# Layer norm, grouped attention and GEGLU on one core: a recorded schedule with clustered half-depth passes, a ones column in V, and the attention output transposed by DMA

## The chip, the cores and the metric

One core of one Trainium2 chip. The metric is the device time of one execution in microseconds. A ratio compares a kernel with the kernel before, by fast runs of the same rounds on the same chip; it is not quite the ratio of the medians that are quoted beside it. The kernel before itself falls into two groups of executions, near 632 and near 635.5 us, so a single ratio is good to about 0.4%, some 2 us. Traces give a span from first to last instruction, which is some 2 us shorter than the device time.

The profiles shorten the names of the engines: PE is TensorE (matmuls; PEld its weight loads), ACT ScalarE, DVE VectorE, POOL GpSimd, SP SyncE. Both kernels let TensorE write its results into PSUM banks of 128 x 512 and have another engine copy a bank out before it is written again. A pitch is the time from the start of one matmul to the start of the next.

## The reference

```python
x  = A_x                                   # 1 x 2048 x 448, bf16
xn = layernorm(x)                          # no weights
q  = (xn @ wq)                             # 448 -> 16 heads x 256
k, v = last 512 of 2048 cached positions   # 8 kv heads, each used by two q heads
p  = softmax(q k^T / 16)                   # no mask
s  = (p v) @ wo                            # 4096 -> 448
b  = (gelu_tanh(xn @ w_gate) * (xn @ w_up)) @ w_down   # 448 -> 1792 -> 448
out = x + s * silu(b)
```

448 is three full contractions of 128 rows and one of 64. The remainders of 64 are done two at a time, on the upper and lower half of the array: a half-depth pair.

## The kernel before

Two stages: the feed-forward (56 units of 128 hidden columns by 512 tokens), then attention (64 steps of one head by 512 tokens). A feed-forward unit on TensorE:

```python
def gate_up(n):
    ...
    for kt in range(nk_full):            # 3 full-depth passes for gate, 3 for up
        pe.matmul(G[n % 2], lhsT=wg[:, kt, cols], rhs=xnT[:, kt, toks], ...)
    ...
    pe.matmul(G[n % 2], lhsT=wg[:HALF, kt, cols], rhs=xnT[:HALF, kt, toks], ...)   # half-depth pair
    pe.matmul(U[n % 2], lhsT=wu[HALF:, kt, cols], rhs=xnT[HALF:, kt, toks], ...)
# then down(n - 3): four matmuls of 448 columns
```

GELU is written as g * sigmoid(2k(g + c g^3)): ACT copies both banks and takes a sigmoid, DVE does four operations a unit. In attention the output is kept feature-major (oT), so the softmax divisor has to be spread over all partitions. POOL sums the exponentials, TensorE multiplies the sum by ones, DVE inverts a whole bank:

```python
pool.tensor_tensor(esum2, expT[0:2], expT[2:4], ALU.add); pool.tensor_tensor(esum, ...)
pe.matmul(DEN[:, :], lhsT=ones[:, :], rhs=esum[:, b, :])          # 512 columns, each head
pe.matmul(O[e], lhsT=vv[:, g, j, e * P:(e + 1) * P], rhs=expT[:, b, j, :], ...)   # 8 per head
dve.reciprocal(rden[:, b, :], DEN[:, :])
dve.tensor_tensor(oT_buf[:, c, :], O[e], rden[:, b, :], ALU.mult)
```

At the start POOL waits for the last x, then issues w_gate, w_up and w_down, and TensorE waits for all of them:

```python
pool.wait_ge(s_xl[last_slot0], 16)
...                                      # w_gate, w_up, w_down
pe.wait_ge(s_wgu, 16 * n_wgu); pe.wait_ge(s_wd, 16); pe.wait_ge(s_tpe, NT)
```

The softmax here doesn't subtract the row's maximum and nothing guards it: scores larger than these inputs give would overflow.

Of the kernel before, what the change touches and what calls it, by code (L numbers as in the profile page):

```python
# [6 lines left out]
ALU = mybir.AluOpType  # L7
# [3 lines left out]
GELU_C = 0.044715  # L11
GELU_SQ_SCALE = GELU_C ** 0.5
GELU_K = 2.0 * 0.7978845608028654
LN_EPS = 1e-5


class _Chain:

    def __init__(self, eng, sem):
        self.eng = eng  # L20
        self.sem = sem
        self.cnt = 0

    def mark(self, ins):
        ins.then_inc(self.sem, 1)
        self.cnt += 1
        return ins

    def wait(self):
        if self.cnt > 0:  # L30
            self.eng.wait_ge(self.sem, self.cnt)


def bass_recurrent_scan__sliding_block_cached__geglu_ffn__prompt_kernel(
# [12 lines left out]
    P = 128  # L47
# [4 lines left out]
    rep = Hq // Hkv  # L52
# [5 lines left out]
    TPC = QC // P  # L58
    kts = []
    o = 0  # L60
    while o < D:
        kts.append((o, min(P, D - o)))
        o += P
    NKT = len(kts)
    NF = F // P
    NJ = W // P
    NE = Dh // P
    NCO = HD // P
    att_scale = float(Dh) ** -0.5
    assert S % QC == 0 and F % P == 0 and W % P == 0 and Dh % P == 0 and D <= 512  # L70
    assert TPC == 4 and NF >= 3 and Hq >= 3

    _cnt = [0]

    def _nm(pfx):
        _cnt[0] += 1
        return "%s_%d" % (pfx, _cnt[0])

    es = ExitStack()
    with es:  # L80
        def sb(stack, shape, dt):
            return stack.enter_context(nc.sbuf_tensor(_nm("sb"), shape, dt))

        def ps(stack, shape, dt):
            return stack.enter_context(nc.psum_tensor(_nm("ps"), shape, dt))

        def new_sem():
            return es.enter_context(nc.semaphore(_nm("sem")))

        ident = sb(es, [P, P], BF16)  # L90
        ones = sb(es, [P, P], BF16)
        xnT = sb(es, [P, NKT, S], BF16)
        gbuf = sb(es, [P, NT, D], BF16)
        wq = sb(es, [P, NKT, HD], BF16)
        wo = sb(es, [P, NCO, D], BF16)
        kT = sb(es, [P, Hkv, NE, W], BF16)
        vv = sb(es, [P, Hkv, NJ, Dh], BF16)

        s_const = new_sem()
        s_xl = [new_sem() for _ in range(16)]  # L100
        s_wgu = new_sem()
        s_wd = new_sem()
        s_wq = new_sem()
        s_w2p = new_sem()
        s_kT = new_sem()
        s_mv = new_sem()
        s_std = new_sem()
        s_xn = new_sem()
        s_tp = new_sem()
        s_tpe = new_sem()  # L110
        s_gu = new_sem()
        s_sq = new_sem()
        s_cp = new_sem()
        s_t1 = new_sem()
        s_sg = new_sem()
        s_act = new_sem()
        s_dn = new_sem()
        s_sig = new_sem()
        s_g = new_sem()
        s_q = new_sem()  # L120
        s_qT = new_sem()
        s_sT = new_sem()
        s_exp = new_sem()
        s_esum = new_sem()
        s_den = new_sem()
        s_rden = new_sem()
        s_oT = new_sem()
        s_oev = new_sem()
        s_s = new_sem()
        s_xr = [new_sem() for _ in range(4)]  # L130
        s_fin = new_sem()
        s_out = [new_sem(), new_sem()]
        s_dve_self = new_sem()
        s_pool_self = new_sem()
        dch = _Chain(nc.vector, s_dve_self)
        pch = _Chain(nc.gpsimd, s_pool_self)
# [3 lines left out]
        x_view = A_x.rearrange("b (t p) d -> p (b t) d", p=P)  # L140
        out_view = out.rearrange("b (t p) d -> p (b t) d", p=P)
        nfull = sum(1 for (_, ksz) in kts if ksz == P)
        kpart = [(kt, ko, ksz) for kt, (ko, ksz) in enumerate(kts) if ksz < P]
        PACK = len(kpart) == 1 and kpart[0][2] * 2 == P and kpart[0][0] == NKT - 1
        HALF = P // 2

        with ExitStack() as e1:
            NXB = min(NT, 16)
            XPAIR = 4
            assert NXB % XPAIR == 0 and NT % XPAIR == 0  # L150
            NXN = 4
            stats = sb(e1, [P, NT, 6], F32)
            mv = sb(e1, [P, NT, 2], F32)
            std = sb(e1, [P, NT], F32)
            rstd = sb(e1, [P, NT], F32)
            eps_c = sb(e1, [P, 1], F32)
            xn2 = sb(e1, [P, NXN, D], BF16)
            wg = sb(e1, [P, NKT, F], BF16)
            wu = sb(e1, [P, NKT, F], BF16)
            wd = sb(e1, [P, NF, D], BF16)  # L160
            NB = 3
            gs = sb(e1, [P, NB, QC], BF16)
            us = sb(e1, [P, NB, QC], BF16)
            q2 = sb(e1, [P, NB, QC], BF16)
            t1 = sb(e1, [P, NB, QC], BF16)
            sg = sb(e1, [P, NB, QC], BF16)

            G = [ps(e1, [P, QC], F32) for _ in range(2)]
            U = [ps(e1, [P, QC], F32) for _ in range(2)]
            Dp = [ps(e1, [P, QC], F32) for _ in range(2)]  # L170


            @blk.gpsimd
            def _(pool):
                pch.mark(pool.memset(ident[:, :], 0.0))
                pch.wait()
                pool.affine_select(
                    out=ident[:, :],
                    in_=ident[:, :],
                    compare_op=ALU.not_equal,  # L180
                    fill=1.0,
                    base=0,
                    pattern=[[-1, P]],
                    channel_multiplier=1,
                ).then_inc(s_const, 1)
                pool.memset(ones[:, :], 1.0).then_inc(s_const, 1)
                pool.memset(eps_c[:, :], LN_EPS).then_inc(s_const, 1)
                if not PACK:
                    for kt, ko, ksz in kpart:
                        pool.memset(xnT[ksz:, kt, :], 0.0).then_inc(s_const, 1)  # L190
                        pool.memset(wg[ksz:, kt, :], 0.0).then_inc(s_const, 1)
                        pool.memset(wu[ksz:, kt, :], 0.0).then_inc(s_const, 1)
                        pool.memset(wq[ksz:, kt, :], 0.0).then_inc(s_const, 1)
                last_slot0 = (min(NT, NXB) - 1) - (min(NT, NXB) - 1) % XPAIR
                pool.wait_ge(s_xl[last_slot0], 16)
                for kt, (ko, ksz) in enumerate(kts):
                    pool.dma_start(wg[:ksz, kt, :], B_w_gate[ko:ko + ksz, :]).then_inc(s_wgu, 16)
                for kt, (ko, ksz) in enumerate(kts):
                    pool.dma_start(wu[:ksz, kt, :], B_w_up[ko:ko + ksz, :]).then_inc(s_wgu, 16)
                if PACK:  # L200
                    kt, ko, ksz = kpart[0]
                    pool.dma_start(wu[ksz:, kt, :], B_w_up[ko:ko + ksz, :]).then_inc(s_wgu, 16)
                pool.dma_start(
                    wd[:, :, :], B_w_down.rearrange("(f p) d -> p f d", p=P)
                ).then_inc(s_wd, 16)
                pool.wait_ge(s_xn, NT)
                pool.wait_ge(s_wd, 16)
                for kt, (ko, ksz) in enumerate(kts):
                    pool.dma_start(wq[:ksz, kt, :], A_wq[ko:ko + ksz, :]).then_inc(s_wq, 16)
                if PACK:  # L210
                    kt, ko, ksz = kpart[0]
                    pool.dma_start(wq[ksz:, kt, :], A_wq[ko:ko + ksz, :]).then_inc(s_wq, 16)
                for g in range(Hkv):
                    pool.dma_start(
                        vv[:, g, :, :],
                        A_v_cache[0, g, Sk - W:Sk, :].rearrange("(j p) d -> p j d", p=P),
                    ).then_inc(s_w2p, 16)
                pool.dma_start(
                    wo[:, :, :], A_wo.rearrange("(c p) d -> p c d", p=P)
                ).then_inc(s_w2p, 16)  # L220

            n_const = 3 + (0 if PACK else 4 * len(kpart))
            n_w2p = Hkv + 1
            n_wq = NKT + (1 if PACK else 0)
            n_wgu = 2 * NKT + (1 if PACK else 0)

            with ExitStack() as eA:
                TP = [ps(eA, [P, 1024], BF16) for _ in range(2)]
                x4 = sb(eA, [P, NXB, D], BF16)
                @blk.sync  # L230
                def _(sp):
                    def xload(t):
                        if t >= NXB:
                            sp.wait_ge(s_xn, t - NXB + XPAIR)
                        sl = t % NXB
                        sp.dma_start(x4[:, sl:sl + XPAIR, :], x_view[:, t:t + XPAIR, :]).then_inc(s_xl[sl], 16)

                    for t in range(0, NT, XPAIR):
                        xload(t)
# [533 lines left out]
```

## Time and profile before

| | before |
|---|---|
| time, median of 4 runs | 635.85 us (631.75 to 636.17) |
| span of the trace | 632.8 us |
| TensorE busy | 595.7 us, 94% |
| first feed-forward matmul | 29.76 us |
| feed-forward unit, head | 2.48 us, 5.39 us |

From the page: busy time by engine, the slices (tenths of 40 slices), and the chain that ended last.

```profile
PE 595.7 (94%) x2818; PEld 256.5 (41%) x2864; DVE 461.4 (73%) x516; ACT 320.9 (51%) x591; POOL 226.7 (36%) x160
...
PE   3499899998969999999999999999999999999897
...
PEclk9999999999999999999999999999999999999989
...
PE 89%; DMA 3%; DVE 3%; ACT 2%; issue 1%; POOL 1%; SPq 0%
```

TensorE is the limit nearly everywhere except in the first slices. DVE at 73% is not: what counts is which engine the chain passes through (the chain of waits that ends last, followed back from the end), and that is DVE for 3% of the span.

The timeline of TensorE in a steady unit (start us, us, what, count; the second number overlaps the next line, so read the starts):

```profile
46.71 0.39 PE L382 MATMUL ps<-sb 64*128 64x512 bf16 x1
46.71 0.39 PE L384 MATMUL ps<-sb 64*128 64x512 bf16 x1
47.03 0.93 PE L395 MATMUL ps<-sb 128*128 128x448 bf16 x4
47.80 0.81 PE L374 MATMUL ps<-sb 128*128 128x512 bf16 x3
48.44 0.81 PE L378 MATMUL ps<-sb 128*128 128x512 bf16 x3
49.19 0.39 PE L382 MATMUL ps<-sb 64*128 64x512 bf16 x1
```

From 46.71 to 49.19 is one unit, 2.48 us. Three full matmuls take 0.64 us before the next group, but the three of L378 (48.44) are followed by the half-depth pair only after 0.75 us, and the pair (46.71) is followed after 0.32 us instead of about 0.215. Those two gaps of about 0.107 us stand where the array goes to 64-row mode and back. The Trainium skill ("TensorEngine Tiling (Array Packing)", Key Properties) says that changing the tiling mode drains TensorE; the trace agrees and gives the price, and experiment 5 tests it.

The costliest DVE and POOL groups (busy us, mean ns, idle before and releaser):

```profile
L682 POOL TENSOR_TENSOR sb<-sb 128x1024 bf16<-128x1024 bf16 x64 | 135.4, 2116 | 346.1 <-ACT sb L663 346.1
L708 DVE RECIPROCAL sb<-ps 128x512 f32<-128x512 f32 x64 | 214.9, 3357 | 57.9 <-PE ps L590 57.9
```

These are large, and almost wholly off the chain: the reciprocal waits for TensorE, and it makes 1% of the chain (POOL another 1%).

### The profile page before, as it was taken

The numbers are of one execution on the slowest core, as the hardware profiler recorded it, in microseconds if no ns is written. First come the engines' busy times: TensorE is split into PE (matmuls) and PEld (weight loads), VectorE is DVE, ScalarE is ACT, GpSimd is POOL, SyncE is SP. The second block draws the span as 40 slices with busy tenths as digits, with TensorE's granted clock in tenths as the row PEclk, the third lists the DMA queues.
The fourth block names the chain that finished last, engine by engine and source line by source line (L and its number), as shares of the span: only waits on it lengthen the run. The fifth ranks groups of instructions, "written<-read, shape, count | busy, mean of one in ns | idle before, by whom it ended". The sixth has DMA issues, their size and how long they took to land.

```text
span 632.8 us, 7556 instructions
## 1 busy us (share of the span) xinstructions
PE 595.7 (94%) x2818; PEld 256.5 (41%) x2864; DVE 461.4 (73%) x516; ACT 320.9 (51%) x591; POOL 226.7 (36%) x160
## 2 busy tenths in 40 slices
PE   3499899998969999999999999999999999999897
PEld 1234343333324444445444444444444444444343
DVE  6378898988838888852888884288888428888942
ACT  3366665767665665511556651155565116556400
POOL 4150000000026666520666662066666206666600
PEclk9999999999999999999999999999999999999989
DMA  7899500000010000001000000100000010000000
GB/s 217 233 306 319 125 1 1 1 2 0 2 29 1 1 2 0 1 16 36 8 1 1 1 0 16 39 6 1 1 1 1 15 41 6 0 1 0 2 8 22
DMA packets 18548, 23.10 MB, mean 37 GB/s; under 512 B 9664, under 2 KB 15840, under 8 KB 18000
## 3 DMA queue, kind: packets, MB, share of 16 engines
q0 software_dynamic: 3088, 15.01, 7.7%
q1 hardware_dynamic: 15424, 7.61, 4.8%
q8 instruction: 23, 0.38, 0.2%
q14 instruction: 13, 0.11, 0.1%
HBM read 18.68 MB, written 1.84 MB: 32 GB/s over the span
## 4 chain that ended last, share of the span: by engine, by line
PE 89%; DMA 3%; DVE 3%; ACT 2%; issue 1%; POOL 1%; SPq 0%
PE ps L597 17%; PE ps L572 17%; PE ps L620 15%; PE ps L531 13%; PE ps L395 7%; PE ps L378 5%; PE ps L374 5%; PE ps L541 3%; PE ps L590 3%; PE ps L382 3%; DMA sb<-in_B_w_down_dram 2%; DVE sb L708 1%; DMA sb<-in_A_x_dram 1%; DVE sb L477 1%; ACT sb L434 1%
## 5 line engine op out<-in xcount | busy, mean ns | idle before, releaser
L682 POOL TENSOR_TENSOR sb<-sb 128x1024 bf16<-128x1024 bf16 x64 | 135.4, 2116 | 346.1 <-ACT sb L663 346.1
L708 DVE RECIPROCAL sb<-ps 128x512 f32<-128x512 f32 x64 | 214.9, 3357 | 57.9 <-PE ps L590 57.9
L663 ACT ACTIVATE sb<-ps 128x512 bf16<-128x512 f32 x256 | 138.9, 594 | 186.4 <-PE ps L572 186.4
L572 PE MATMUL ps<-sb 128*128 128x512 bf16 x480 | 124.6, 379 | 4.7 <-ACT sb L653 2.9
L597 PE MATMUL ps<-sb 128*128 128x512 bf16 x512 | 122.5, 383 | 0.5 <-DVE sb L713 0.3
L531 PE MATMUL ps<-sb 128*128 128x512 bf16 x383 | 103.5, 379 | 0.5
L620 PE MATMUL ps<-sb 128*128 128x448 bf16 x512 | 97.7, 353 | 0.0
L713 DVE TENSOR_TENSOR sb<-ps,sb 128x512 bf16<-128x512 f32 x128 | 82.5, 686 | 2.2
L653 ACT ACTIVATE sb<-ps 128x512 bf16<-128x512 f32 x128 | 69.4, 594 | 20.3 <-PE ps L546 20.3
L572 PEld LDWEIGHTS ps<-sb 128*128 128x128 bf16 x512 | 49.4, 97 | 64.8 <-ACT sb L663 12.0
L689 POOL TENSOR_TENSOR sb<-sb 128x512 bf16<-128x512 bf16 x64 | 73.8, 1154 | 5.0
L597 PEld LDWEIGHTS ps<-sb 128*128 128x128 bf16 x512 | 50.4, 99 | 54.6 <-issue 2.0
L620 PEld LDWEIGHTS ps<-sb 128*128 128x128 bf16 x512 | 50.2, 98 | 47.4 <-issue 0.8
L721 DVE TENSOR_TENSOR sb<-ps,sb 128x448 f32<-128x448 f32 x16 | 10.0, 625 | 71.2 <-PE ps L620 71.2
L395 PE MATMUL ps<-sb 128*128 128x448 bf16 x224 | 51.9, 355 | 6.8 <-DVE sb L477 4.6
L418 ACT ACTIVATE sb<-ps 128x512 bf16<-128x512 f32 x56 | 33.4, 597 | 46.5 <-PE ps L384 46.5
L531 PEld LDWEIGHTS ps<-sb 128*128 128x128 bf16 x384 | 37.6, 98 | 45.2
L453 DVE SCALAR_TENSOR_TENSOR sb<-sb 128x512 bf16<-128x512 bf16 x56 | 38.7, 690 | 23.2 <-ACT sb L419 23.0
L374 PE MATMUL ps<-sb 128*128 128x512 bf16 x159 | 44.6, 387 | 5.1 <-DMA sb<-in_B_w_down_dram 4.9
L378 PE MATMUL ps<-sb 128*128 128x512 bf16 x164 | 46.5, 388 | 0.4
L458 DVE SCALAR_TENSOR_TENSOR sb<-sb 128x512 bf16<-128x512 bf16 x56 | 38.8, 692 | 1.9
L424 ACT ACTIVATE sb<-sb 128x512 bf16<-128x512 bf16 x56 | 35.4, 632 | 1.3 <-DVE sb L458 1.0
(48 smaller groups left out, 378.1 us busy)
## 6 DMA issues: line engine op xcount, KB each, us to landing
sb<-in_A_wo_dram POOLq DMA_DIRECT2D x1, 3584.0 KB, 27.1
sb<-in_A_wq_dram POOLq DMA_DIRECT2D x3, 1024.0 KB, 7.9
sb<-in_A_v_cache_dram POOLq DMA_DIRECT2D x8, 256.0 KB, 15.3
sb<-in_A_x_dram SPq DMA_DIRECT2D x4, 448.0 KB, 4.9
sb<-in_A_x_dram SPq DMA_DIRECT2D x16, 112.0 KB, 2.1
out_dram<-sb SPq DMA_DIRECT2D x16, 112.0 KB, 1.7
sb<-in_B_w_down_dram POOLq DMA_DIRECT2D x1, 1568.0 KB, 15.3
sb<-in_B_w_gate_dram POOLq DMA_DIRECT2D x3, 448.0 KB, 4.5
```

The costliest lines, as they stand in the source:

```text
L374: pe.matmul(G[n % 2][:, :], lhsT=wg[:, kt, cols], rhs=xnT[:, kt, toks], start=(kt == 0), stop=(kt == NKT - 1))
L378: ins = pe.matmul(U[n % 2][:, :], lhsT=wu[:, kt, cols], rhs=xnT[:, kt, toks], start=(kt == 0), stop=(kt == NKT - 1))
L395: ins = pe.matmul(Dp[t4][:, 0:D], lhsT=actT[:, f, t4 * P:(t4 + 1) * P], rhs=wd[:, f, :], start=(f == 0), stop=(f == NF - 1),)
L531: ins = pe.matmul(Q[e][:, :], lhsT=wq[:, kt, h * Dh + e * P:h * Dh + (e + 1) * P], rhs=xnT[:, kt, toks], start=(kt == 0), stop=(kt == NKT ...
L572: ins = pe.matmul(Sb[c % 2][:, :], lhsT=kT[:, g, e, j * P:(j + 1) * P], rhs=qTb[:, b, e, :], start=(e == 0), stop=(e == NE - 1),)
L597: ins = pe.matmul(O[e][:, :], lhsT=vv[:, g, j, e * P:(e + 1) * P], rhs=expT[:, b, j, :], start=(j == 0), stop=(j == NJ - 1),)
L620: ins = pe.matmul(bank[:, 0:D], lhsT=oT_buf[:, c, t4 * P:(t4 + 1) * P], rhs=wo[:, c, :], start=(c == 0), stop=(c == NCO - 1),)
L663: act.activation(expT[:, b, j, :], Sb[c % 2][:, :], ACT.Exp, scale=att_scale).then_inc(s_exp, 1)
L682: pch.mark(pool.tensor_tensor(esum2[:, b, :], expT[:, b, 0:2, :].rearrange("p j q -> p (j q)"), expT[:, b, 2:4, :].rearrange("p j q -> p ( ...
L689: pool.tensor_tensor(esum[:, b, :], esum2[:, b, 0:QC], esum2[:, b, QC:2 * QC], ALU.add).then_inc(s_esum, 1)
L708: dve.reciprocal(rden[:, b, :], DEN[:, :]).then_inc(s_rden, 1)
L713: dve.tensor_tensor(oT_buf[:, c, :], O[e][:, :], rden[:, b, :], ALU.mult).then_inc(s_oev, 1)
```

## The change

The intent is to take work and gaps from TensorE and to start it earlier. The file is rewritten around a recorder: operations are recorded with the buffers they read and write, and the waits are derived. The order per engine is the order of recording. Core of the diff, cut:

```diff
-# each unit: 3 + 3 full passes, then its own half-depth pair
+gu_full(n, 0, True); gu_full(n + 1, 2, True)          # two units, full depth
+ln_more()                                             # normalise one more x tile
+gu_rem(n, 0, False); gu_evac(n, 0)                    # four half-depth pairs together
+gu_rem(n + 1, 2, False); gu_evac(n + 1, 2)
+gu_rem(n + 2, 4, True); gu_rem(n + 3, 6, True)
+gu_full(n + 2, 4, False); gu_evac(n + 2, 4)           # two units, full depth
+ln_more()
+gu_full(n + 3, 6, False); gu_evac(n + 3, 6)
+if sg == 1:                                           # loads, issued by POOL
+    ... load_wq(i) (12 DMAs), load_v(g) (8 DMAs)
 ... (the projection of q likewise, in clusters of four heads)

-act copies G and U, sigmoid; dve four operations
+act(gl, bank[b], ACT.Gelu_apprx_tanh)
+dve.tensor_tensor(actT, bank[b + 1], gl, ALU.mult)

-pool sums, ones matmul, 512-column reciprocal, oT = O * rden
+va[:, :, :, Dh:VW] = 1.0                              # ones beside V; VW = Dh + 2
+for t4 in range(4):                                   # token-major output
+    matmul(bank[4 + t4][:, 0:Dh + 1], lhsT=expT[:, x, j, t4 * P:(t4 + 1) * P], rhs=va[:, g, j, 0:Dh + 1])
+    dve.reciprocal(rden, bank[4 + t4][:, Dh:Dh + 1])  # 128 x 1
+    dve.tensor_scalar(onorm, bank[4 + t4][:, 0:Dh], rden, ALU.mult)
+dma_start_transpose(oT[...], onorm[...])              # per pair of heads and 128 tokens

-std on ACT (Sqrt), reciprocal on DVE, PE transposes of all 16 tiles before the first matmul
+rstd = (var + eps) ^ -0.5 on POOL; four tiles first (PE transposes), twelve during feed-forward (DMA)
+first 512 columns of w_gate and w_up loaded by ACT at once; w_down waited for only before the first down block
```

The down matmuls now come in four blocks of 56, one for each 512 tokens, some groups after the units that feed it. exp takes two banks at a time (1024 columns), and silu is written with tanh instead of sigmoid.

## The prediction

> What bounds it now. TensorE: the busy table has it at 94%, the chain of waits at 89%, the clock row at full speed. The timeline gives exact pitches: 213 ns for a 512-column matmul[...]. A feed-forward unit (six full matmuls, one half-depth pair, four down matmuls) repeats every 2.48 us; its matmuls are 2.24. The rest is two gaps of 0.107 us, where the array goes to half-depth (64 row) matmuls and where it returns. The Trainium skill ("TensorEngine Tiling (Array Packing)", Key Properties) says that a change of tiling mode drains the array; the trace agrees, with 0.107 us each. An attention head repeats every 5.39 us: 24 slots (5.12), two gaps (0.21). Output projection: 24.2 us per query chunk, four times. The first feed-forward matmul starts at 29.8 us, behind the w_down load; full pitch only from about 40 us.
>
> TensorE time removed:
> - Denominator matmul with ones: 64 x 0.213 = 13.7 us. The ones column makes PV 1024 matmuls of 257 columns; at column pitch 107 ns, 109.7 us against 109.2 now. Their 1024 weight loads should hide: the timeline shows those of the transposes 0.06 us apart.
> - Mode gaps: 120 pairs become 30 (14 in the feed-forward, 16 in attention): 90 x 0.213 = 19 us.
> - Start: after needs only four x tiles, their normalisation and the first 512 columns of the weights; I estimate the first matmul at 12 us instead of 29.8.
> - Waits at the feed-forward/attention boundary (180 to 188 us, 3 us) and before the last output projection, where POOL's sum, the reciprocal and a half-rate clock cost about 5 us (600 to 605 us).
>
> Moved, off the chain: the 512-column reciprocal (3.36 us, 215 us of DVE in all) becomes 128x1 reciprocals and 256-column scalings, estimated 3 us of DVE per head of about 4.9 us; POOL's 209 us of sums vanish; GELU needs one ACT pass and one DVE multiply. ACT exp becomes 1024 wide, estimated 1.05 us, under 3 us per head.
>
> Added: 128 transposes of the output by DMA, and 12 for the normalised input. The skill ("Advanced Engine Details and Errata", X-Bar Transpose) calls transposing DMAs as fast as plain ones; this trace shows nine issued in 16.2 us, 1.8 us per 128 KB, or 73 GB/s. Four per head pair are 7.2 us against about 9.8 us of TensorE, so they fit; before each output projection there are 7.7 us of other matmuls.
>
> Sum: feed-forward 83.6 + 41.8, attention 95.6 (Q) + 109.2 (scores) + 109.7 (PV) + 95.6 (output), gaps 6: 542 us. Plus start 12, cold clock 2, early stalls 7 (second weight part lands late; POOL waits for DMA slots before normalising later tiles, which holds DVE), small gaps 6, end 4: 573 us.
>
> Predicted: 573 us, 8 in 10 between 560 and 592. Faster by over 2%: 0.97; within: 0.025; slower: 0.005.
>
> Signs. Right: TensorE 95% or more of the span; PV pitch about 0.107 us; first feed-forward matmul before 14 us; POOL under 5%; no wait of TensorE on transposes; about 30 pairs of gaps. Wrong: PV pitch near 0.13 us (+20 us: weight loads bound it); TensorE waiting for transposes at output projections (several us, four times); TensorE waiting for weight loads or DVE during the first 45 us over 10 us in sum; DVE behind in PV, TensorE waiting for scalings.
>
> Most likely to break it: PV pitch, transpose rate from SBUF, early stalls.

## The result, and the profile after

| | before | after |
|---|---|---|
| time, median of 4 | 635.85 us | 585.93 us (585.56 to 586.64) |
| span of the trace | 632.8 us | 583.7 us |
| first feed-forward matmul | 29.76 us | 11.30 us |
| TensorE busy | 94% | 96% |

The ratio is 0.925, 95% interval 0.921 to 0.929. The same lines of the page:

```profile
PE 559.8 (96%) x3260; PEld 300.8 (52%) x3260; DVE 274.3 (47%) x729; ACT 205.1 (35%) x270; POOL 43.1 (7%) x85
...
PE   3939999999999999999999999999999999999997
...
PEclk9978999999999999999999999999999999999999
...
PE 92%; POOL 3%; DMA 2%; DVE 1%; ACT 1%; issue 0%; SPq 0%; DVEq 0%
```

DVE lost 187 us and POOL 184 us of busy time and the span lost 49: time off the chain counts for little. There is a hole in the third slice, with a lower clock behind it. The timeline of TensorE there:

```profile
31.55 0.81 PE L308 MATMUL bank<-xnT,wg 128*128 128x512 bf16 x3
42.09 1.46 PE L308 MATMUL bank<-xnT,wu 128*128 128x512 bf16 x3 [9.74 <-DVE actT L445]
43.35 1.49 PE L308 MATMUL bank<-xnT,wg 128*128 128x512 bf16 x3
```

TensorE stood 9.74 us for DVE, and afterwards three matmuls took 1.28 us (43.35 to 44.63), twice the 0.65 of full speed, until about 47.7 us. The Trainium skill ("TensorE: Matmul & The Clock Gate", Part 1) says that the clock falls to half after a few microseconds of idleness and recovers after a few of work; this trace agrees. What DVE and POOL did then:

```profile
41.02 0.41 DVE L358 TENSOR_SCALAR xn<-x_65,mv,rstd 128x512 bf16<-128x512 bf16 x1 [12.32 <-POOL rstd L353]
41.35 1.88 DVE L445 TENSOR_TENSOR actT<-bank,gl 128x512 bf16<-128x512 f32 x3
...
26.78 7.33 POOL L293 DMA_DIRECT2D wq<-in_A_wq_dram  x12
34.10 5.97 POOL L293 DMA_DIRECT2D va<-in_A_v_cache_dram  x8
40.09 0.24 POOL L351 TENSOR_SCALAR ve<-mv 128x1 f32<-128x1 f32 x1
```

DVE waited 12.32 us for the 128x1 rstd of one tile, because POOL issued 20 DMAs first, 13.3 us back to back. In the recorded order the three operations of L445, which empty PSUM banks, come after this xn; they ran only at 41.35, and TensorE, out of banks, went on at 42.09.

One cluster of four heads, TensorE:

```profile
303.17 5.12 PE L308 MATMUL bank<-xnT,wq 128*128 128x512 bf16 x26
308.13 1.89 PE L308 MATMUL bank<-qT,kT 128*128 128x512 bf16 x8
309.86 1.46 PE L308 MATMUL bank<-xnT,wq 128*128 128x512 bf16 x6
311.15 1.89 PE L308 MATMUL bank<-qT,kT 128*128 128x512 bf16 x8
312.88 1.95 PE L308 MATMUL bank<-va,expT 128*128 128x257 bf16 x16
314.67 1.89 PE L308 MATMUL bank<-qT,kT 128*128 128x512 bf16 x8
316.39 1.95 PE L308 MATMUL bank<-va,expT 128*128 128x257 bf16 x16
318.18 1.89 PE L308 MATMUL bank<-qT,kT 128*128 128x512 bf16 x8
319.90 3.80 PE L308 MATMUL bank<-va,expT 128*128 128x257 bf16 x32
```

The starts show no wait; the next cluster begins at 323.54, so four heads take 20.37 us, against 4 x 5.39 = 21.56 before. Sixteen PV matmuls take 1.79 us, 0.112 us each.

### The profile page after: what moved, and what is told of

Same layout as the page of the kernel before. It is cut to its first block, busy times and chain, and to the rows that moved or that the text cites. A ratio compares the mean times of both kernels' runs of the same rounds, so it can differ in the third digit from the quotient of the medians.

```text
span 583.7 us, 8116 instructions
## 1 busy us (share of the span) xinstructions
PE 559.8 (96%) x3260; PEld 300.8 (52%) x3260; DVE 274.3 (47%) x729; ACT 205.1 (35%) x270; POOL 43.1 (7%) x85
## 4 chain that ended last, share of the span: by engine, by line
PE 92%; POOL 3%; DMA 2%; DVE 1%; ACT 1%; issue 0%; SPq 0%; DVEq 0%
PE bank L308 92%; DMA wu<-in_B_w_up_dram 1%; POOL wq L293 1%; POOL va L293 1%; DMA x_65<-in_A_x_dram 1%; DVE actT L445 0%; POOL rstd L353 0%; DVE stats L349 0%; ACT L299 0%; ACT gl L299 0%; ACT expT L299 0%; POOL wg L293 0%; POOL ve L351 0%; SPq L293 0%; DVE xn L358 0%
## 5 line engine op out<-in xcount | busy, mean ns | idle before, releaser
L299 ACT ACTIVATE expT<-bank 128x1024 bf16<-128x1024 f32 x128 | 124.0, 1021 | 145.9 <-PE bank L308 145.9
L546 DVE TENSOR_SCALAR onorm<-bank,rden 128x256 bf16<-128x256 f32 x256 | 123.8, 484 | 9.3 <-DVE rden L544 0.3
L308 PE MATMUL bank<-va,expT 128*128 128x257 bf16 x1024 | 123.4, 273 | 0.0
L308 PE MATMUL bank<-qT,kT 128*128 128x512 bf16 x512 | 121.1, 379 | 1.1 <-ACT expT L299 1.0
L308 PEld LDWEIGHTS bank<-va,expT 128*128 128x128 bf16 x1024 | 98.4, 98 | 27.2 <-DVE onorm L546 3.0
L308 PE MATMUL bank<-xnT,wq 128*128 128x512 bf16 (+1 forms) x512 | 105.1, 379 | 0.0
L308 PE MATMUL bank<-wo,oT 128*128 128x448 bf16 x512 | 97.5, 352 | 0.0
L308 PEld LDWEIGHTS bank<-wo,oT 128*128 128x128 bf16 x512 | 50.1, 98 | 46.8
L308 PE MATMUL bank<-xnT,wu 128*128 128x512 bf16 (+2 forms) x230 | 61.8, 386 | 10.0 <-DVE actT L445 9.7
L308 PE MATMUL bank<-xnT,wg 128*128 128x512 bf16 (+2 forms) x230 | 61.6, 385 | 0.0
L445 DVE TENSOR_TENSOR actT<-bank,gl 128x512 bf16<-128x512 f32 x56 | 36.9, 687 | 27.7 <-ACT gl L299 21.9
L308 PEld LDWEIGHTS bank<-xnT,wu 128*128 128x128 bf16 (+1 forms) x230 | 21.7, 100 | 30.6 <-DVE actT L445 10.2
```

What stands on the lines that cost most here:

```text
L299: K.op("act", lambda e, o=o, i=i: e.activation(o, i, func, scale=scale), reads, writes)
L308: ins = e.matmul(o, lhsT=l, rhs=r, start=st, stop=sp)
L445: K.op("dve", lambda e: e.tensor_tensor(actT[:, c % 2, f, :], bank[b + 1], gl[:, s, :], ALU.mult), (b_ps[b + 1], b_gl[s]), (b_actT[c % 2][ ...
L546: K.op("dve", lambda e, bb=bb, r=r, t4=t4: e.tensor_scalar(onorm[:, o, t4, h % 2, :], bank[bb][:, 0:Dh], rden[:, r:r + 1], None, op0=ALU.m ...
```

## The experiments

Twelve kernels ran; all gave correct results except a_pv256. "Over the late loads" below means: against the kernel of the second experiment, by the quotient of the two ratios to the kernel before. By their intervals such a quotient is good to about 0.5%, some 3 us; medians are given beside it.

### 1. More DMA slots for POOL (a_slots40)

```diff
-    SLOTS = {"sp": 16, "act": 8, "pool": 16}
+    SLOTS = {"sp": 16, "act": 8, "pool": 40}
```

> The changed kernel with 40 DMA semaphore slots for POOL instead of 16, so that no load of POOL ever waits for an older load to land. If the stop of TensorE at 31.6 to 42.1 us comes from slot waits (the prediction's reason), the stop shrinks by most of its 9.7 us and the time falls to about 575 us. If it comes from the time that POOL needs to issue the 20 loads of wq and v (7.33 + 5.97 us in the timeline, back to back), nothing changes: 586 us within 1.5 us, and the stop stays at 9 to 10 us.

Measured: 586.05 us (585.35 to 587.09), unchanged. TensorE's wait was 10.2 us, and POOL took as long as before for the same twenty issues:

```profile
27.10 7.35 POOL L293 DMA_DIRECT2D wq<-in_A_wq_dram  x12
34.44 5.98 POOL L293 DMA_DIRECT2D va<-in_A_v_cache_dram  x8
```

The prediction had foreseen a stall through this very path, but with POOL waiting for slots. That is refuted: it is the issue time, 0.61 us for a part of wq and 0.75 us for one of v. Experiment 2 moves it.

### 2. Loads after the last normalisation (a_late_loads)

```diff
-            if sg == 1:
+            if sg == 5:
                 for i in range(Hq // 4):
                     load_wq(i)
                 ...
```

> The changed kernel with the issue of the wq and v loads moved from after feed-forward group 1 to after group 5, when the last tile has been normalised. Both theories of the stop (slot waits, issue time) expect it to vanish: TensorE waits for DVE under 1 us in the first 50 us, no half clock after 42 us, time 573 to 575 us (9.7 us of wait and about 2.5 us of half clock less). If the stop came from the x tiles or from DVE's own work, it stays and the time stays at 586 us.

Measured: 575.0 us (573.74 to 575.43), ratio 0.906 to before. The clock stays full, and of TensorE's wait for DVE in the feed-forward, 9.7 us, 0.9 us is left. The place of these 20 DMA issues in POOL's order cost 11 us. In the slices, TensorE's longest wait for DVE there, and POOL's timeline (its window ends at 60 us; all twelve took 7.35 us):

```profile
PE   3999999999999999999999999999999999999997
...
PEclk9999999999999999999999999999999999999999
...
41.53 0.39 PE L308 MATMUL bank<-xnT,wg 64*128 64x512 bf16 x1 [0.44 <-DVE actT L445]
...
53.52 0.57 POOL L353 TENSOR_TENSOR rstd<-ve,nhalf 128x1 f32<-128x1 f32 x1
54.04 6.31 POOL L293 DMA_DIRECT2D wq<-in_A_wq_dram  x10
```

The issues take as long as they did, but now stand after the last rstd.

### 3. and 4. The pitch of PV (a_pv256, a_vrow544)

```diff
-    bank[bb][:, 0:Dh + 1], ..., va[:, g, j, 0:Dh + 1]      # a_pv256, wrong on purpose
+    bank[bb][:, 0:Dh], ..., va[:, g, j, 0:Dh]
```
```diff
-    VW = Dh + 2                                            # a_vrow544, right
+    VW = Dh + 16
```

> Wrong results on purpose: PV has 256 columns instead of 257, and the divisor is read from a value column. In the changed kernel a PV matmul takes about 0.112 us from start to start, where 257 columns at the pitch of the 512-column matmuls would be 0.107. If a fixed cost of each short matmul (or of its weight load) is the reason, 16 matmuls still take about 1.78 us and the time falls by under 1 us. If the odd column (257, or the row that ends in the middle of a word) is the reason, 16 take 1.71 us and the time falls by about 5 us.

> The changed kernel with rows of V of 544 bytes instead of 516, so that every moving operand of PV begins on a multiple of 32 bytes; still 257 columns. If the start of the rows is the reason for the PV pitch of 0.112 us, 16 matmuls fall to about 1.71 us and the time by about 5 us. If a fixed cost per short matmul is the reason, nothing changes (within 1 us).

Measured: 584.95 us and 584.97 us, each about 1 us less than the changed kernel (586.05 us, as a_slots40). From start to start 16 PV matmuls took 1.77 us with 256 columns and 1.76 us with 257 columns and wide rows, against 1.79 us. Neither gives 1.71. So most of the excess is a fixed cost for each matmul (or for its weight load; no run separates the two). The Trainium skill ("TensorE: Matmul & The Clock Gate", Back-to-back issue gap) gives N / 2.4 + 2.5 ns for a warm array, as the gap of an isolated matmul. For 257 columns that is 109.6 ns, and 1.76 us / 16 is 110. The other 2 ns of the 112 go away with rows of 544 bytes: from one start to the next, the median over the PV matmuls of the whole trace is 112 ns in the changed kernel and 110 ns with wide rows. The kernel's time is too coarse to prove so small a part; it rests on one trace of each.

### 5. Half-depth passes not clustered (a_unclustered)

```diff
-gu_full(n), gu_full(n+1), gu_rem(n), gu_rem(n+1), gu_rem(n+2), gu_rem(n+3), gu_full(n+2), gu_full(n+3)
+gu_full(n), gu_rem(n), gu_full(n+1), gu_rem(n+1), gu_full(n+2), gu_rem(n+2), gu_full(n+3), gu_rem(n+3)
 # the evacuation follows each unit's last pass; q_full and q_rem likewise; late loads
```

> The changed kernel with the late loads (575 us), and the half-depth passes not clustered: each feed-forward unit and each head does its full passes and then its own half-depth pair. 120 pairs of changes of mode instead of 30. If each pair costs 0.213 us of TensorE, as the gaps in the trace of before say, the time rises by 19 us to about 594 us. If the queue hides most of it (the rival: clustering is tidiness), it rises by under 5 us.

Measured: 592.34 us, ratio to before 0.936. Over the late loads that is 0.936 / 0.9063 = 1.033, 19 us; by medians 17.3 us. A cluster of four heads became 0.64 us longer (303.26 to 324.27 us, 21.01 against 20.37), three pairs of changes at 0.213 us. The clustering is worth what the gaps in the trace of before said.

```profile
303.26 5.22 PE L308 MATMUL bank<-xnT,wq 128*128 128x512 bf16 x24
...
324.27 1.02 PE L308 MATMUL bank<-xnT,wq 128*128 128x512 bf16 x4
```

### 6. Transposes on TensorE (a_pe_transpose, a_pe_transpose2)

```diff
-dma_t(oT[:, 4 * p:4 * p + 4, t4 * P:(t4 + 1) * P], onorm[:, o, t4, :, :], ...)
+for k in range(4):                       # through the PV bank of this t4, after the next scores
+    e.transpose(tp[:, k * P:(k + 1) * P], onorm[:, o, t4, k // 2, ...], ident)
+act(oT[...], tp[...], ACT.Copy)          # a_pe_transpose2: DVE for t4 = 0 and 2, ACT for 1 and 3
```

> The changed kernel with the late loads (575 us), and the 128 transposes of the attention output done by TensorE (512 transposes of 128x128 through the PV banks, copied out by ACT) instead of by DMA. Estimate: 512 x 0.06 us = 31 us more on TensorE, and some microseconds for the last four, which stand before the last output projection: about 608 us. If instead the copies on ACT (128 x 0.6 us = 77 us) or the banks hold TensorE up, it is over 620 us. If TensorE had slack, under 590 us.

Measured: 634.23 us, ratio 1.002: as slow as the kernel before. Over the late loads 1.106. The estimate of 608 us was wrong, as was the size of the copies' part:

```profile
307.70 1.06 PE L559 MATMUL bank<-ident,onorm 128*128 128x128 bf16 x16
309.52 3.88 PE L308 MATMUL bank<-va,expT 128*128 128x257 bf16 x32 [0.76 <-ACT oT L299]
```

The 16 transposes take about the time that was estimated (0.065 us each); then TensorE waits for ACT to empty the bank. With the copies on two engines:

> The kernel of the previous transposes on TensorE (634 us, 59 us over the late loads), with the copies out of the banks split between ACT and DVE instead of all on ACT. In that run 16 transposes took 1.06 us of TensorE and then TensorE waited 0.76 us for the first copies, in each of the 32 groups. If the loss beyond the transposes' own time (32 x 1.06 = 34 us) is that wait for copies, two engines halve it: 615 to 625 us. If it lies elsewhere (bank order, changes of mode), the time stays at 634 us.

Measured: 615.04 us, ratio 0.970. The wait in that place fell from 0.76 to 0.29 us:

```profile
302.12 1.06 PE L559 MATMUL bank<-ident,onorm 128*128 128x128 bf16 x16
...
303.94 3.31 PE L308 MATMUL bank<-va,expT 128*128 128x257 bf16 x28 [0.29 <-ACT oT L299]
```

So of the 59 us by which the first version was slower, 19 us were the copies on one engine (TensorE's listed waits for these copies fell from 21.1 to 4.7 us). The remaining 40 us are about 30 to 34 us of transposes (32 groups, 0.9 to 1.06 us each) and what waits are left. On DMA the same work costs TensorE nothing that the trace shows: no wait of TensorE on a transposing DMA stands in the list of waits of the changed kernel.

### 7. One more matmul per head (a_extra_matmul)

```diff
+mms([(bank[4], ones[:, :], expT[:, x, 0, :], True, True)])   # overwritten by the first PV matmul
 for t4 in range(4):
     ... PV
```

> The changed kernel with the late loads (575 us), and one more matmul of 512 columns with ones for each head (its result is overwritten), so that TensorE does again the work of the denominator matmul that the ones column replaced. If TensorE is the limit in all of attention, the time rises by 64 x 0.213 = 13.7 us to about 589 us. If the heads wait for something else, it rises by less.

Measured: 588.08 us, ratio 0.929; over the late loads 1.025, 14.5 us (13.1 us by medians). One matmul of TensorE's time per head is a matmul of the kernel's time: attention is limited by TensorE without slack, so the denominator's removal was worth its full price. What replaced it was not free: PV took 64 x 1.72 = 110.1 us before and takes 115.5 us now, so the net gain is about 8 us.

```profile
307.18 0.38 PE L311 MATMUL bank<-expT,ones 128*128 128x512 bf16 x1
307.39 1.95 PE L311 MATMUL bank<-va,expT 128*128 128x257 bf16 x16
```

### 8. The native GELU: alone in the kernel before (b_gelu), and taken out of the kernel after (a_poly_gelu)

```diff
-act.activation(gs, G, ACT.Copy); act.activation(us, U, ACT.Copy); ... sigmoid; dve: four operations
+act.activation(gs, G, ACT.Gelu_apprx_tanh)                   # b_gelu
+dve.tensor_tensor(actT[:, f, :], U[n % 2], gs, ALU.mult)
```
```diff
-act(gl, bank[b], ACT.Gelu_apprx_tanh); dve: one multiply     # a_poly_gelu, with the late loads
+act: copy, copy, sigmoid; dve: g*g*c, (q+1)*g, s*g, *u       # skewed by one unit, as before had it
```

> The kernel before with the native tanh-GELU alone: one ACT pass and one DVE multiply in a feed-forward unit in place of three ACT passes and four DVE operations (the sigmoid of the gate stays, so the ACT tables are swapped eight times more). In the kernel before TensorE is busy without gaps in steady feed-forward (2.48 us a unit against 2.2 us of DVE), so if the GELU lies off the chain, the ratio to before is 0.99 to 1.00. If it lies on the chain, the unit gets shorter than 2.48 us and the ratio is below 0.98.

> The changed kernel with the late loads (575 us) and the sigmoid form of GELU of the kernel before back in place of the native one (three ACT passes, four DVE operations a unit; two x tiles buffered at the end instead of four, to make room). In the kernel before the native GELU alone gave nothing. There a unit had 2.48 us; here the groups of four units take 6.26 us, 1.57 a unit, and the down matmuls come in blocks. If GELU still lies off the chain, 575 to 578 us. If it has become the limit of the feed-forward groups (2.23 us of DVE a unit against 1.57), the time rises by 20 to 35 us, to 595 to 610 us, and TensorE waits for DVE in the groups.

Measured: b_gelu 633.52 us, ratio 1.000 (0.997 to 1.004), with TensorE's unit still at 2.48 us (61.14 to 63.62; its seven more table loads, 10 against 3, made no hole there):

```profile
61.14 0.39 PE L382 MATMUL ps<-sb 64*128 64x512 bf16 x1
...
63.62 0.39 PE L382 MATMUL ps<-sb 64*128 64x512 bf16 x1
```

a_poly_gelu 613.13 us, ratio 0.967; over the late loads 1.067, 38 us. That is a little more than expected. TensorE waits for ACT's copies out of the banks, ACT for DVE's polynomial (gl_t), and the clock falls in the holes (mean 0.976; the slices show 7 to 8 tenths in the feed-forward):

```profile
ACT gl_t L301 <- DVE gl_t L468: 46.2, 44, 2.8
PE bank L310 <- ACT gl_us L301: 20.6, 11, 2.8
...
PEclk9977798999999999999999999999999999999999
```

The same exchange is worth nothing in one kernel and 38 us in the other. In the kernel before, a unit gave DVE 2.48 us for 2.2 us of GELU. The changed order gives it 6.26 / 4 = 1.57 us, mainly because the four down matmuls of a unit (0.77 us, 47.03 to 47.80) have gone into blocks of their own; the gaps saved by clustering are about 0.16 us of the 0.91. DVE also normalises twelve tiles there. That DVE and not ACT sets the pace is what the waits suggest; ACT's three passes (1.8 us a unit) exceed 1.57 us too, and no run took them away alone.

### 9. Only looser waits for the loads, in the kernel before (b_loads)

```diff
-pool.wait_ge(s_xl[last_slot0], 16)          # weights no longer wait for x
-pe.wait_ge(s_wd, 16)                        # at the start of the feed-forward
+if n == 0: pe.wait_ge(s_wd, 16)             # before the first down matmul
```

> The kernel before with only the order of its loads loosened: the weight loads no longer wait for x, and TensorE waits for w_down only before the first down matmul. First feed-forward matmul at about 18 to 22 us instead of 29.8 us, ratio to before 0.983 to 0.99 (7 to 11 us less). If the start was bound by normalisation and transposes rather than by w_down, it starts at 24 us or later and the ratio is above 0.99.

Measured: 640.13 us, ratio 1.010 (1.006 to 1.015): slower by 1%, which is clear of noise. The first expectation was wrong; the second ("24 us or later", above 0.99) holds by its numbers, but did not foresee a later start than before: 35.56 us instead of 29.76. The weight loads, issued earlier, delayed those of x, as the median time of an x load to landing shows (9.3 us instead of 4.9), and DVE waited:

```profile
15.50 2.21 DVE L259 BATCH_NORM_STATS2 sb<-sb 128x6 f32<-128x448 bf16 x4 [2.29 <-DMA sb<-in_A_x_dram]
17.75 0.38 DVE L263 BATCH_NORM_AGGREGATE sb<-sb 128x2 f32<-128x6 f32 x4
25.63 2.21 DVE L259 BATCH_NORM_STATS2 sb<-sb 128x6 f32<-128x448 bf16 x4 [7.51 <-DMA sb<-in_A_x_dram]
```

Fewer waits alone therefore gain nothing at the start. The changed kernel also asks for less: four x tiles and 512 weight columns come first. This run tests a rougher change than that, so how the 18 us split between order and size stays open.

### 10. All mends together (a_best)

```diff
-            if sg == 1:                      # wq and v loads
+            if sg == 6:
-    VW = Dh + 2
+    VW = Dh + 16
+    ln_norm of tile t - 1 before ln_stats of tile t          # DVE does not wait for POOL
+    act(ve[:, 1:2], ve[:, 0:1], ACT.Exp)     # after the units: the table of Exp is loaded early
```

> The changed kernel with four mends: the wq and v loads after group 6; statistics of a tile one step ahead of its normalisation, so that DVE does not stand 1.07 us for POOL; rows of V of 544 bytes; the table of Exp loaded before the last down block. From the runs: 575 us of the late loads, minus 1 (rows, measured), minus 1.3 (table load that TensorE waited for), minus about 2 (waits for DVE in groups 3 to 5): about 571 us, ratio 0.898 to 0.905.

Measured: 571.41 us (570.75 to 571.95), ratio to before 0.902. It is the fastest of all; the changed kernel itself has 585.93 us. TensorE is busy 98% of the span. How the last 3.6 us split among the smaller mends was not measured separately (only the wide rows were, 1 us).

## Why the prediction was right, point by point

The prediction was 573 us (560 to 592); the time was 585.9 us, 13 us more. The main mechanism held: TensorE is the limit, and what leaves TensorE leaves the time. The 13 us are about 5 us of stalls beyond the allowance, about 5 us of matmul pitch beyond the small gaps, 1.4 us of a wait for exp, and 2 us between a span and a device time. That an allowance stood at the place of the stall was partly luck, since its reason was wrong. The sum, term by term, from the starts in the trace of the changed kernel:

| term | predicted us | measured us |
|---|---|---|
| gate and up, with gaps | 83.6 + 3.0 | 14 groups x 6.26 = 87.6 |
| down | 41.8 | 4 x 10.60 = 42.4 |
| Q with gaps | 95.6 + 3.4 | 16 x (4.96 + 1.29) = 100.0 |
| scores | 109.2 | 16 x 6.90 = 110.4 |
| PV | 109.7 | 16 x 7.22 = 115.5 |
| output projection | 95.6 | 4 x 24.2 = 96.8 |
| small gaps | 6 | in the lines above |
| start | 12 | 11.3 |
| cold clock and early stalls | 2 + 7 | 133.4 - 87.6 - 31.8 = 14.0 (first matmul to the end of the units) |
| first wait for exp | 0 | 1.4 |
| end | 4 | 3.8 |
| sum | 573 | 583.2, for a span of 583.7 |

- **Denominator, 13.7 us**: right. Putting the matmul back cost 13 to 14.5 us. The longer PV (below) takes some 5 us of it back.
- **Mode gaps, 19 us**: right. Unclustering cost 17 to 19 us.
- **Start, 12 us**: right (11.30), and experiment 9 shows that looser waits alone would not have given it.
- **Waits at the boundary, 3 us, and before the last output projection, 5 us**: right. Of the first 1.4 us is left; the last output projection follows PV without a wait (551.89 to 555.53).
- **Reciprocal, sums, GELU off the chain**: right for the kernel before. The prediction did not say that the changed order, with the down matmuls in blocks, makes GELU's cheapness a condition; experiment 8 showed it.
- **Transposes by DMA fit**: right. TensorE never waited for them. Their landing took 2.5 us at the median, and each held SP's queue for 1.27 us, not the estimated 1.8: that figure was the mean of nine k transposes, of which one took 5.8 us beside other loads and the others 1.3.
- **Early stalls, 7 us plus 2 of cold clock**: the right place, the wrong reason and too small. It was 20 issues on POOL, not waits for slots, and the stall brought a half-rate clock with it: 14.0 us in all, of which moving the loads gave back 11.
- **PV pitch 0.107 us**: too small. It was 0.112 us, 5.8 us over all. The pitch of 213 ns for 512 columns was too small as well. It can rest on three matmuls in 0.64 us, too short a stretch to be exact; eight in 1.72 us are 215 ns, and from one start to the next the median in both traces is 216 ns. For 448 columns it is 189 ns (56 in 10.60 us), where the sums used 187. So 2 to 3 ns per matmul were lost, which the allowance of 6 us for small gaps covered only in part.
- The prediction summed spans and compared them with device times, a difference of some 2 us.
- **POOL under 5%** was a sign that failed: 7%; the sixteen rstd (9.1 us) and the DMA issues make up most of its 43.1 us.
- **A sign of "wrong" was met**, or stood on its border: TensorE's waits for weight loads or DVE in the first 45 us, over 10 us in sum. They were 9.74 and 0.26 us after the first feed-forward matmul, and 9.1 us before it. The time stayed in the range all the same.

## What to carry to other kernels

When one engine is the limit without slack, count its slots and gaps exactly, from start to start in a steady stretch, and the sum can hold to a few per cent, as here (2%); most of what was missing lay in equal parts in the first 50 us and in 2 to 5 ns per matmul. Keep a burst of DMA issues off an engine while it still has to produce a small value that the engine emptying PSUM waits for: here that cost 11 us. Whether a cheaper operation is worth anything depends on the interval that the order gives it, so judge it in the schedule where it will stand: here 0 us in one and 38 us in the other.

## What the Trainium skill lacked or had wrong

- "TensorEngine Tiling (Array Packing)", Key Properties, says that a change of tiling mode drains TensorE but not what it costs: 0.107 us each way in the trace of before (0.213 us for a pair, confirmed by 17 to 19 us for 90 pairs).
- "DMA: Bandwidth & Descriptors" gives first-byte latencies but, that I found, no figure for the time for which POOL itself is occupied by issuing: 0.61 us for each of 12 DMAs of wq and 0.75 us for each of 8 of v. Their sum, 13.3 us, was the cause of the largest stall.
- "Advanced Engine Details and Errata", X-Bar Transpose, calls DMA transposes as fast as regular DMAs. By the time to landing the changed kernel agrees: 2.5 us for 128 KB transposed within SBUF, 2.3 us for a plain load of 112 KB. SP's queue spent 34.0 us on eight transposes of 256 KB in the changed kernel (62 GB/s) and 16.2 us on nine of 128 KB in the kernel before (73 GB/s), but these are not their rates: single ones took from 1.3 to 11.1 us, the long ones while the DMA engines were also full with other loads. Where mostly transposes were left (90 to 101 us of the changed kernel), full DMA engines moved 143 to 194 GB/s, against 251 to 309 GB/s from 15 to 44 us, with mostly plain loads; this is one trace, and what slows them is not shown.
- "TensorE: Matmul & The Clock Gate", Back-to-back issue gap, was right with N / 2.4 + 2.5 ns (257 columns: 109.6 against 110 measured with wide rows), which it calls the gap of an isolated matmul. Its other figure there, about 131 ns for N = 512 in a sustained stream, was not seen in any trace here: 215 to 216 ns. It lacks that rows of 516 bytes cost a 257-column matmul some 2 ns more than rows of 544 (112 against 110 ns, one trace each).
